# Attention's product with the values turned round, and its row sums taken by a column of ones

## The chip, the cores and the metric

The kernel runs on one core of one Trainium2 chip. A core has a matrix engine (TensorE, PE in the profile, with its weight loads listed as PEld), a vector engine (VectorE, DVE), a scalar engine (ScalarE, ACT), a general engine (GpSimd, POOL), a synchronisation engine that here only issues transfers (SyncE, SP), and 16 DMA engines that move data between the chip's memory and the core's SBUF. Results of TensorE land in PSUM, of which this kernel uses all eight banks (2 KB for each of 128 partitions). Each engine works through its own list of instructions in order; across engines an instruction waits for what it needs by semaphores. The metric is the device time of one execution, in microseconds. All data here are float32.

## The reference: what is computed

The reference is an attention with a band and a few global keys, followed by a mixture of eight experts in which each token goes to one expert:

```python
# B, H, S, D = 4, 8, 768, 64; n_global, n_local = 8, 96
scores = scale * q @ k.T                       # per batch and head
keep   = (pos_k < n_global) | (0 <= pos_q - pos_k < n_local)
dist   = where(global and not local, n_local, |pos_q - pos_k|)
scores = where(keep, scores - slope[h] * dist, -1e9)
a = exp(scores - max); a = a / sum(a)
x = (a @ v) as (B*S, H*D)                      # 3072 tokens of 512 numbers
logits = x @ w_gate                            # 512 x 8
e = argmax(logits); g = softmax(logits)[e]
y = g * relu(x @ w1[e]) @ w2[e]                # 512 x 1024 and 1024 x 512
```

## The kernel before

**Stages.** Three stretches follow one another: the attention of four batches (about 11 to 161 us of the profile), a tail in which the last tokens are routed while the first tokens of expert 0 are already worked on (161 to 217 us), and the other experts' matrix products (217 to 509 us). The order in each engine's list is the order in which the program is written: nothing reorders it.

**Units and rounds.** A *unit* is one batch `b`, one pair of heads `j` (four pairs) and two tiles of 128 queries (`c` = 0, 1, 2): 48 units, 12 a batch. A query tile sees only its own key block and one other (`kA`, the block before, with the 16 first keys in place of its first 16), so a unit has four 128x128 blocks of scores for each head (three where `c` is 0). The loop takes two units a *round*. In a round the lists get: `turn_qk` (VectorE's 32x32 transposes for the next pair of heads, L462), `scores` of both units (TensorE `s` L508; the exponential on ScalarE L514 into `e`; the product with the weights of distance on VectorE L521 and L525), `turn` of the units of two rounds before, `attend` of the units of the round before, now and then a step of the routing, then ScalarE's copies that make the next pair's shifted keys (`keys_at`, L427, L429) and values (`turn_v`, L453, L454), and the loads of later pairs (`load`, `load_v`), which SP issues.

**`attend` and `turn`.** `attend` multiplies with the exponentials `e` as the stationary operand and the values as the moving one. The values carry a column of ones, so that the sum of each row of `e` comes out beside the product; the moving operand is 128 columns wide, of which the 65 first are used. VectorE takes the reciprocals of the sums (L547), multiplies (L550) and so leaves finished `x` in `xr`, token by row. `turn` transposes `xr` on TensorE (`px`, L560), ScalarE copies the result (L562) into `w2_f`, a stretch of SBUF that later holds expert 1's second weights, and once a pair of heads is the last, `store` (L252) writes the rows of `x` to the table `x_tok` in the chip's memory, from which the experts gather their tokens.

**Routing.** Once a batch, in the round with `m` = 2 of the next batch (`m` counts units within a batch): `logits` multiplies the transposed `x` by the gate matrix on TensorE (`pq`, L574, in column groups of 32), VectorE transposes, `gate` finds each token's expert, with one exponential on ScalarE (`ex`, L233). `spread` (a product `pr` with a triangle of ones), `tables` (VectorE: `oh`, L624) and `spread_sum` (`pi`, L633) turn this into each token's place in its expert's list; they follow at `m` = 4, 6 and 8, or 4, 4 and 6 for the last batch that the loop serves.

**The tail.** After the loop the last batch goes through the same steps. Between them `work(1)` puts a piece of expert 0's product (`ph` L346 with its relu L341, and `po` L354) into TensorE's list, so that it has something to do while VectorE routes. Expert 0's weights (`w_first`; L760 and L762) are loaded by SP in pieces, one at a time from unit 12 on; expert 1's 4 MB (`w_second`, in whose place attention keeps its operands) are issued by SP in the tail. GpSimd gathers the rows of `x_tok` by index for each expert.

**PSUM.** `ps_s` holds the scores (two tiles of two banks), `ps_o` the product (two of one bank), `ps_m` everything else (two of one bank).

## Time and profile before

| | |
|---|---|
| time, median of 3 runs | 518.11 us (517.02 to 518.5) |
| the profiled execution, its own time | 518.61 us |
| its span in the profile | 516.7 us |
| granted TensorE clock, mean | 0.996 |
| TensorE busy | 500.3 us, 97% |
| weight loads (beside TensorE) | 346.6 us, 67% |
| VectorE busy | 181.4 us, 35% |
| ScalarE busy | 127.4 us, 25% |
| GpSimd busy | 137.9 us, 27% |
| TensorE busy of the attention's 150 us (11 to 161) | 148.6 us |
| VectorE, ScalarE busy in the same stretch | 121.0 us, 89.7 us |
| TensorE busy of the tail's 56 us (161 to 217) | 55.9 us |
| TensorE busy of the experts' 292 us (217 to 509) | 291.1 us |
| memory read, written | 59.0 MB, 12.75 MB |

The span runs from the first to the last instruction that the profile shows; 1.9 us of the execution's own time lie around it. The experts' stretch keeps TensorE at work all the time, and so do the attention and the tail. TensorE's records overlap, because its products are pipelined; a float32 product is two records ("x2"). In the lines shown below, the chain of the work that ended last has a start and a duration, the engine, the output's name, the line and the number of records; the timeline has a start, a duration, the engine, the line, the operation, the output and inputs with their sizes, the number of records, and in brackets a wait with what ended it.

### The profile page before, as it was taken

To read this page: it belongs to the slowest core of one execution; us is meant where nothing else is said; L and a number is where in the kernel's file an instruction comes from. 1 tells how busy PE (TensorE), PEld (TensorE's weight loads), DVE (VectorE), ACT (ScalarE), POOL (GpSimd) and SP (SyncE) were. 2 spreads that over 40 slices of the span, in tenths; PEclk is the share of its full clock that TensorE was granted. 3 is DMA by queue.
4 is the path that set the end of the run, shared out by engine and by line. 5 is a ranking of instruction groups with operands and counts; after the bars stand their busy time and mean duration, and the time that the engine had idled before them with its cause. 6 is when DMAs were issued, how large, how long until landed. Compare 5 with 4: busy or idle time off the path is not lost.

```text
span 516.7 us, 7988 instructions
## 1 busy us (share of the span) xinstructions
PE 500.3 (97%) x3108; PEld 346.6 (67%) x3108; DVE 181.4 (35%) x484; ACT 127.4 (25%) x227; POOL 137.9 (27%) x161
## 2 busy tenths in 40 slices
PE   4999999999999999999999999999999999999993
PEld 3999999999999949955455455545545746545541
DVE  5878797897884532310300120030012021020010
ACT  4776656656651102011002001101100201101100
POOL 5000000000024266543353244244025526310010
PEclk9999999999999999999999999999999999999998
DMA  9998999999937911963751826466083576010001
GB/s 153 160 171 154 238 178 172 226 173 171 290 99 215 273 38 45 229 219 71 165 179 62 159 82 203 85 147 210 4 192 88 175 185 213 22 42 18 1 23 41
DMA packets 145183, 71.95 MB, mean 139 GB/s; under 512 B 126672, under 2 KB 126678, under 8 KB 145136
## 3 DMA queue, kind: packets, MB, share of 16 engines
q1 hardware_dynamic: 137344, 58.16, 48.8%
q0 software_dynamic: 5264, 12.59, 8.1%
q10 hardware_dynamic: 2528, 0.59, 0.7%
q8 instruction: 26, 0.43, 0.4%
q14 instruction: 21, 0.17, 0.1%
HBM read 59.00 MB, written 12.75 MB: 139 GB/s over the span
## 4 chain that ended last, share of the span: by engine, by line
PE 87%; POOL 3%; DMA 3%; DVE 3%; issue 2%; SPq 1%; POOLq 0%; ACT 0%
PE ph L1066 28%; PE po L1123 27%; PE o L543 14%; PE s L508 8%; PE px L560 2%; PE ph L346 2%; POOL xq_s L288 2%; DMA xq_s<-x_tok,rows 2%; PE pt L1132 1%; PE po L354 1%; PE pq L574 1%; PE pi L633 1%; DMA w_first<-in_moe_w_dram 1%; PE first L443 1%; SPq L252 0%
## 5 line engine op out<-in xcount | busy, mean ns | idle before, releaser
L1068 ACT ACTIVATE hT<-ph 128x416 f32<-128x416 f32 (+4 forms) x64 | 29.9, 467 | 278.0 <-PE ph L1066 278.0
L334 DVE TENSOR_SCALAR y<-po,gslot_s 128x512 f32<-128x512 f32 (+1 forms) x17 | 12.8, 751 | 215.4 <-PE po L1123 215.4
L288 POOL DMA_INDIRECT xq_s<-x_tok,rows_s x72 | 72.6, 1008 | 58.3 <-ACT hT L1068 42.7
L1066 PE MATMUL ph<-xe,w_second 128*128 128x416 f32 (+3 forms) x256 | 79.4, 470 | 0.3 <-DVE xe L299 0.3
L1123 PE MATMUL po<-w_second,hT 128*128 128x512 f32 (+1 forms) x176 | 76.2, 592 | 0.0
L1066 PE MATMUL ph<-xe,w_first 128*128 128x208 f32 (+3 forms) x256 | 75.8, 457 | 0.1
L1066 PEld LDWEIGHTS ph<-xe,w_second 128*128 128x128 f32 x256 | 48.3, 190 | 29.7 <-issue 10.4
L1066 PEld LDWEIGHTS ph<-xe,w_first 128*128 128x128 f32 x256 | 47.5, 190 | 27.6 <-issue 10.7
L1123 PE MATMUL po<-w_first,hT 128*128 128x512 f32 (+1 forms) x144 | 62.3, 592 | 0.0
L1123 PEld LDWEIGHTS po<-w_second,hT 128*128 128x128 f32 (+1 forms) x176 | 33.2, 189 | 41.3 <-issue 40.7
L288 POOL DMA_INDIRECT xq<-x_tok,rows x15 | 15.7, 1044 | 163.1 <-DVE rows L271 158.0
L543 PE MATMUL o<-vt,e 128*128 128x128 f32 x288 | 53.9, 278 | 0.0
L326 POOL DMA_INDIRECT out_dram<-y,idx_s x17 | 17.2, 1010 | 124.9 <-DVE xe L299 72.0
L1123 PEld LDWEIGHTS po<-w_first,hT 128*128 128x128 f32 (+1 forms) x144 | 27.2, 189 | 34.0 <-issue 33.5
L543 PE MATMUL o<-va,e 128*128 128x128 f32 x240 | 46.9, 277 | 0.0
L543 PEld LDWEIGHTS o<-vt,e 128*128 128x128 f32 x288 | 43.1, 195 | 0.2 <-issue 0.2
L514 ACT ACTIVATE e<-s 128x1024 f32<-128x1024 f32 (+1 forms) x36 | 33.4, 947 | 31.5 <-PE s L508 31.3
L508 PE MATMUL s<-qT,kT 64*128 64x128 f32 x384 | 38.8, 286 | 0.9 <-ACT qT L445 0.9
L543 PEld LDWEIGHTS o<-va,e 128*128 128x128 f32 x240 | 36.9, 194 | 0.1
L508 PE MATMUL s<-qT,kA 64*128 64x128 f32 x320 | 34.2, 292 | 2.0 <-ACT kA L429 2.0
L525 DVE TENSOR_TENSOR e<-e,Wb 128x1024 f32<-128x1024 f32 x24 | 28.8, 1212 | 9.3 <-ACT e L514 9.0
L508 PEld LDWEIGHTS s<-qT,kT 64*128 64x128 f32 x384 | 30.2, 196 | 2.2 <-ACT qT L445 1.3
(189 smaller groups left out, 503.1 us busy)
## 6 DMA issues: line engine op xcount, KB each, us to landing
w_second<-in_moe_w_dram SPq DMA_DIRECT2D x16, 512.0 KB, 8.4
w_second<-in_moe_w_dram SPq DMA_DIRECT2D x4, 2048.0 KB, 9.7
x_tok<-xr SPq DMA_DIRECT2D x24, 256.0 KB, 3.9
w_first<-in_moe_w_dram SPq DMA_DIRECT2D x12, 512.0 KB, 8.6
w_first<-in_moe_w_dram SPq DMA_DIRECT2D x3, 2048.0 KB, 9.9
vt<-in_v_dram SPq DMA_DIRECT2D x31, 192.0 KB, 3.8
w_second<-in_q_dram SPq DMA_DIRECT2D x60, 96.0 KB, 3.3
w_second<-in_k_dram SPq DMA_DIRECT2D x60, 96.0 KB, 2.8
```

The costliest lines, as they stand in the source:

```text
L288: return nc.gpsimd.indirect_dma_start(out=xq[:, i, :], out_offset=None, in_=x_tok[0:NJ * top, :], in_offset=bass.IndirectOffsetOnAxis(ap=c ...
L326: p = nc.gpsimd.indirect_dma_start(out=to[:, :], out_offset=bass.IndirectOffsetOnAxis(ap=where, axis=0), in_=y[0:rows, :], in_offset=None, ...
L334: done = nc.vector.tensor_scalar(out=y[0:rows, :], in0=po[0:rows, :], scalar1=gs[0:rows, :], scalar2=None, op0=ALU.mult)
L346: done = nc.tensor.matmul(ph[:, P * f:P * f + P], lhsT=w1_0[:, 0, kc, c0:c0 + P], rhs=xe_0[:, kc, P * q:P * q + P], start=(kc == 0), stop= ...
L508: nc.tensor.matmul(ps[:, h, P * m:P * m + P], lhsT=lhsT, rhs=qT[r, P * i:P * i + P], start=True, stop=True)
L514: nc.scalar.activation(e[:, :, 0:w], ps[:, :, 0:w], AF.Exp, scale=D ** -0.5)
L525: nc.vector.tensor_tensor(out=eh, in0=eh, in1=W[:, 2 * j:2 * j + 2, P:3 * P].rearrange("p h (o c) -> p h o c", o=1).to_broadcast([P, 2, 2, ...
L543: nc.tensor.matmul(po[:, t, h, :], lhsT=pt[:, h, P * m:P * m + P], rhs=(vt if own else va)[:, c0:c0 + P], start=(m == mine[0][0]), stop=(m ...
L560: nc.tensor.transpose(px[:, 2 * i + t, :], xrs[b, c][:, t, P * j:P * j + P], ident)
L1066: nc.tensor.matmul(ph[:, 0:C], lhsT=w1t[:, 0, kc, P * fc:P * fc + P], rhs=xe[:, kc, 0:C], start=(kc == 0), stop=(kc == KC - 1))
L1068: done = nc.scalar.activation(hT[:, fc, 0:C], ph[:, 0:C], AF.Relu)
L1123: nc.tensor.matmul(po[0:rows, :], lhsT=hT[:, fc, P * q:P * q + rows], rhs=w2t[:, 0, fc, :], start=(fc == 0), stop=(fc == FC - 1))
```

## The change

`attend` is turned round: the values are the stationary operand (64 columns) and `e` the moving one. The two heads of a pair go into the two column halves of the array, so `po` is `x` transposed, 64 rows a head, one after the other by heads; ScalarE copies it into `w2_f` (L550), unscaled. Its PSUM is now one bank for both units of a round (`po_all`), and the bank that this leaves free collects sums (`pc_all`). The row sums come from four further products a unit: a stationary operand of 32 columns (`one_of`, a column of ones at a place that depends on the unit), one of four column quarters for each head and key block, `e` 256 wide; the sums of a whole batch pile up in one bank, one row a unit. `turn` now transposes from `w2_f` to token by row, and two copies of ScalarE bring it into `xr`, still unscaled.

Once a batch ScalarE copies the sums out (`sums_out`), TensorE transposes them into an unused part of the last scores' banks, VectorE adds the two key blocks' shares and takes the reciprocals (`recip_of`). The gate's products are made per pair of heads, with each head's columns apart (`partials`, `pl`), copied to SBUF, transposed back (`pq`), multiplied by the reciprocals and added up (`logits`), and `finish_x` scales the three `xr` of a batch on VectorE and stores them. The loop places these at `m` = 0, 2 and 8 of the next batch (4 for the last that it serves). In the tail the stores come after `tables`, and expert 1's weights after the stores. Expert 0's weights start six units later, and what is left of them is issued after the loop. The values lose their column of ones, and GpSimd the filling of it (these edits aren't in the cut below); token numbers, reciprocals and gate matrix change their layout. Lines of the kernel after: `s` L497, exponential L503, `o_all` L532, `c_all` L548, its copy L550, `px` L557, copies L562, `sums_out` L568, transposes L573, `partials` L587, `pq` L600, `finish_x` L619, expert 0's relu L341.

```diff
-            ps_o = actx.enter_context(tc.tile_pool(name="ps_ob", bufs=2, space=PSUM))
+            ps_o = actx.enter_context(tc.tile_pool(name="ps_ob", bufs=1, space=PSUM))
             ps_m = actx.enter_context(tc.tile_pool(name="ps_mb", bufs=2, space=PSUM))
-
-            VW = D + 1
+            ps_c = actx.enter_context(tc.tile_pool(name="ps_cb", bufs=1, space=PSUM))
+
+            po_all = ps_o.tile([P, 2, 2, P], F32, tag="o", name="o_all")
+            pc_all = ps_c.tile([P, 2, 2, P], F32, tag="c", name="c_all")
...
+            one_of = vp.tile([P, 2 * 32 - 1], F32, name="one_of")
+            nc.vector.memset(one_of, 0.0)
+            nc.vector.memset(one_of[:, 31:32], 1.0)
...
-                po = ps_o.tile([P, 2, 2, P], F32, tag="o", name=f"o_{n}")
+                po = po_all[:, n % 2, :, :]
                 for t in range(2):
                     mine = [(m, own) for m, (u, own) in enumerate(bl) if u == t]
-                    for h in range(2):
-                        for m, own in mine:
-                            i = 2 * c + t
-                            c0 = VT * h + VW * i if own else VA * h + VW * (i - 1)
-                            nc.tensor.matmul(po[:, t, h, :], lhsT=pt[:, h, P * m:P * m + P],
-                                             rhs=(vt if own else va)[:, c0:c0 + P],
-                                             start=(m == mine[0][0]), stop=(m == mine[-1][0]))
-                r = recips[:, 2 * n:2 * n + 2, :]
-                nc.vector.reciprocal(r.rearrange("p t (h o) -> p t h o", o=1), po[:, :, :, D:D + 1])
-                if j == 0:
-                    xrs[b, c] = xrp.tile([P, 2, DM], F32, tag="xr", name=f"xr_{b}_{c}")
-                nc.vector.tensor_tensor(
-                    out=xrs[b, c][:, :, P * j:P * j + P].rearrange("p t (h d) -> p t h d", h=2), in0=po[:, :, :, 0:D],
-                    in1=r.rearrange("p t (h o) -> p t h o", o=1).to_broadcast([P, 2, 2, D]), op=ALU.mult)
+                    for m, own in mine:
+                        i = 2 * c + t
+                        for h in range(2):
+                            nc.tensor.matmul(po[D * h:D * h + D, t, :], lhsT=vt[:, h, i, :] if own else va[:, h, i - 1, :],
+                                             rhs=pt[:, h, P * m:P * m + P], start=(m == mine[0][0]), stop=(m == mine[-1][0]))
+                m = n % nb
+                pc = pc_all[:, b % 2, :, :]
+                r = NJ * c + j
+                for own in (1, 0):
+
+                    lots = [(1, 2)] if c == 0 and not own else [(0, 1), (1, 2)] if m == 1 and not own else [(0, 2)]
+                    for t0, t1 in lots:
+                        for h in range(2):
+                            g = 2 * h + own
+                            if c == 0 and not own:
+                                rhs = pt[:, h, P:2 * P].rearrange("p (t q) -> p t q", t=1)
+                            else:
+                                k = own if c > 0 else 0
+                                rhs = pt[:, h, :].rearrange("p (t k q) -> p k t q", k=2, q=P)[:, k, t0:t1, :]
+                            nc.tensor.matmul(pc[32 * g:32 * g + 32, t0:t1, :], lhsT=one_of[:, 31 - r:63 - r], rhs=rhs,
+                                             start=(m == 0), stop=(m == nb - 1))
+                nc.scalar.copy(out=w2_f[:, 2 * P * m:2 * P * m + 2 * P], in_=po.rearrange("p t q -> p (t q)"))
 
             def turn(n):
 
                 px = ps_m.tile([P, 4, P], F32, tag="m", name=f"px_{n}")
+                for i in range(4):
+                    o = 2 * P * (n % nb) + P * i
+                    nc.tensor.transpose(px[:, i, :], w2_f[:, o:o + P], ident)
                 for i in range(2):
                     b, j, c = units[n + i]
-                    for t in range(2):
-                        nc.tensor.transpose(px[:, 2 * i + t, :], xrs[b, c][:, t, P * j:P * j + P], ident)
-                m = n % nb
-                nc.scalar.copy(out=w2_f[:, 2 * P * m:2 * P * m + 4 * P], in_=px.rearrange("p t c -> p (t c)"))
-                for i in range(2):
-                    b, j, c = units[n + i]
-                    if j == NJ - 1:
-                        store(S * b + 2 * P * c, 2, xrs.pop((b, c)))
+                    if j == 0:
+                        xrs[b, c] = xrp.tile([P, 2, DM], F32, tag="xr", name=f"xr_{b}_{c}")
+                    nc.scalar.copy(out=xrs[b, c][:, :, P * j:P * j + P], in_=px[:, 2 * i:2 * i + 2, :])
+
+            gl = w1_f[:, 4 * S:5 * S].rearrange("p (c t q) -> p c t q", t=2, q=P)
+            sums = w1_f[:, 5 * S:5 * S + 2 * P].rearrange("p (t q) -> p t q", t=2)
+
+            def sums_out(b):
+                nc.scalar.copy(out=sums, in_=pc_all[:, b % 2, :, :])
+
+            def recip_of(b, pr):
+
+                for t in range(2):
+                    nc.tensor.transpose(pr[:, t, :], sums[:, t, :], ident)
+                to = recips[:, b, :, :, :].rearrange("p t c h -> p t (c h)")
+                for t in range(2):
+                    nc.vector.tensor_reduce(
+                        out=to[:, t, :].rearrange("p (r h) -> p h r", h=2),
+                        in_=pr[:, t, :].rearrange("p (h o r) -> p h r o", h=2, o=2)[:, :, 0:nb, :], axis=AX.X, op=ALU.add)
+                nc.vector.reciprocal(to, to)
+
+            def partials(b, c0, c1):
+
+                pl = ps_m.tile([P, c1 - c0, 2 * P], F32, tag="m", name=f"pl_{b}_{c0}")
+                for c in range(c0, c1):
+                    for j in range(NJ):
+                        o = 2 * P * (NB // 2 * j + c)
+                        nc.tensor.matmul(pl[32 * j:32 * j + 32, c - c0, :], lhsT=wg_sb[:, j, :], rhs=w2_f[:, o:o + 2 * P],
+                                         start=True, stop=True)
+                nc.scalar.copy(out=gl[:, c0:c1, :, :].rearrange("p c t q -> p c (t q)"), in_=pl)
 
             def logits(b):
 
-                xl = w2_f[:, 0:KC * S].rearrange("p (k t) -> p k t", k=KC)
-                pq = ps_m.tile([P, QS], F32, tag="m", name=f"pq_{b}")
-                for kc in range(KC):
-                    for g in range(TB):
-                        nc.tensor.matmul(pq[32 * g:32 * g + 32, :], lhsT=wg_sb[:, kc, :], rhs=xl[:, kc, QS * g:QS * g + QS],
-                                         start=(kc == 0), stop=(kc == KC - 1))
-                L = gp.tile([P, QS], F32, tag="L", name=f"L_{b}")
-                nc.vector.transpose(L, pq)
-                gate(b, L.rearrange("p (c w) -> p c w", w=32)[:, :, 0:E], gp,
-                     M_b[b][:, :, 1:NB + 1].rearrange("p e c -> p c e"))
+                tmp = gp.tile([P, NB * P], F32, tag="oh", name=f"tmp_{b}", bufs=1)[:, 0:NB * H * E].rearrange(
+                    "p (i h e) -> p i h e", h=H, e=E)
+                tiles = [(t, c) for t in range(2) for c in range(NB // 2)]
+                for i0, i1 in ((0, 4), (4, NB)):
+                    pq = ps_m.tile([P, i1 - i0, NJ, 32], F32, tag="m", name=f"pq_{b}_{i0}")
+                    for i in range(i0, i1):
+                        t, c = tiles[i]
+                        nc.tensor.transpose(pq[:, i - i0, :, :].rearrange("p j w -> p (j w)"), gl[:, c, t, :], ident)
+                    n = (i1 - i0) * NJ
+                    r = recips[:, b, :, :, :].rearrange("p t c (j h) -> p (t c j) h", h=2)
+                    nc.vector.tensor_tensor(
+                        out=tmp[:, i0:i1, :, :].rearrange("p i (j h) e -> p (i j) h e", h=2),
+                        in0=pq.rearrange("p i j w -> p (i j) w")[:, :, 0:2 * E].rearrange("p n (h e) -> p n h e", h=2),
+                        in1=r[:, NJ * i0:NJ * i1, :].rearrange("p n (h o) -> p n h o", o=1).to_broadcast([P, n, 2, E]), op=ALU.mult)
+                L = gp.tile([P, NB, E], F32, tag="L", name=f"L_{b}")
+                nc.vector.tensor_reduce(out=L, in_=tmp.rearrange("p i h e -> p i e h"), axis=AX.X, op=ALU.add)
+                gate(b, L, gp, M_b[b][:, :, 1:NB + 1].rearrange("p e c -> p c e"))
                 nc.vector.tensor_tensor_scan(out=C_b[b].rearrange("p e c -> p (e c)"), data0=first0.rearrange("p e c -> p (e c)"),
                                              data1=M_b[b].rearrange("p e c -> p (e c)"), initial=0.0, op0=ALU.mult, op1=ALU.add)
                 if b < B - 1:
                     nc.vector.tensor_copy(out=M_b[b + 1][:, :, 0:1], in_=C_b[b][:, :, NB:NB + 1])
...
+            def finish_x(b, c):
+
+                xr = xrs.pop((b, c))
+                x4 = xr.rearrange("p t (h d) -> p t h d", h=H)
+                nc.vector.tensor_tensor(out=x4, in0=x4, in1=recips[:, b, :, c, :].rearrange("p t (h o) -> p t h o", o=1)
+                                        .to_broadcast([P, 2, H, D]), op=ALU.mult)
+                store(S * b + 2 * P * c, 2, xr)
...
-                    if n % 3 > 0 and n >= 12:
+                    if n % 3 > 0 and n >= 18:
...
+                if b > 0 and m == 0:
+                    partials(b - 1, 0, 1)
+                if b > 0 and m == 2:
+                    recip_of(b - 1, st["ps"][:, :, 3 * P:4 * P])
+                    partials(b - 1, 1, NB // 2)
                 if n0 >= 4:
                     turn(n0 - 4)
                     for n in two:
                         attend(n - 2)
                         if n == nu - 4:
                             fetch_0(0)
+                if b > 0 and m == 0:
+                    sums_out(b - 1)
                 if b > 0 and m == 2:
                     logits(b - 1)
                 if b > 0 and m == 4:
                     spread(b - 1)
+                if b > 0 and m == (4 if b == B - 1 else 8):
+                    for i in range(NB // 2):
+                        finish_x(b - 1, i)
...
             attend(nu - 2)
             turn_x(xe_0, xq_0[0], TB)
+            partials(B - 1, 0, 1)
             turn(nu - 4)
             attend(nu - 1)
+            sums_out(B - 1)
             turn_x(xe_0[:, :, P:2 * P], xq_0[1], TB)
+            while weights_0:
+                weights_0.pop(0)()
+            st["ph"], st["po"] = (ps_s.tile([P, 2, 512], F32, tag="s", name=f"{i}_0") for i in ("ph", "po"))
             work(1)
             count_0()
+            recip_of(B - 1, st["ph"][:, 0, 2 * P:4 * P].rearrange("p (t q) -> p t q", t=2))
             turn(nu - 2)
-            expert_w1(w1_1, slice(1, 2))
+            partials(B - 1, 1, NB // 2)
             work(1)
             logits(B - 1)
-            nc.sync.dma_start(w2_1, w2v[:, 1:2, :, :])
+            finish_x(B - 1, 0)
             work(1)
             spread(B - 1)
             tables(B - 1)
+            for i in range(1, NB // 2):
+                finish_x(B - 1, i)
+            expert_w1(w1_1, slice(1, 2))
+            nc.sync.dma_start(w2_1, w2v[:, 1:2, :, :])
```

## The prediction

> **What bounds the kernel now.** First the busy sums, then the chain that ended last, because a busy TensorE is not yet a TensorE at its rate.
>
> ```profile
> PE 500.3 (97%) x3108; PEld 346.6 (67%) x3108; DVE 181.4 (35%) x484; ACT 127.4 (25%) x227; POOL 137.9 (27%) x161
> ```
>
> In the chain (start, duration) one round of two units is scores `s`, transposes `px`, products `o`:
>
> ```profile
> 52.55 3.13 PE o L543 x28
> 55.67 1.44 PE pq L574 x32
> 57.11 1.99 PE s L508 x32
> 59.09 0.58 PE px L560 x4
> 59.68 3.13 PE o L543 x28
> ...
> 261.68 1.88 PE pt L1132 x64
> ```
>
> The rows meet end to end and TensorE has no waits of weight after 24 us: the attention stage (about 11 to 161 us) runs at TensorE's rate. A float32 product is two records (passes). `o` takes 3.13/28 = 0.112 us a pass; `s`, whose two heads lie in different row halves, two passes in 0.112; `pt`, four column quarters, four passes in 1.88/16 = 0.118. So products in different parts of the array run together.
>
> The TensorE timeline of one round shows the price of changing from one partition of the array to another:
>
> ```profile
> 124.63 0.39 PE L543 MATMUL o<-vt,w_second 128*128 128x128 f32 x2
> 124.95 0.49 PE L508 MATMUL s<-qT,kA 64*128 64x128 f32 x4
> 125.28 0.39 PE L508 MATMUL s<-qT,kT 64*128 64x128 f32 x4
> ...
> 126.39 0.39 PE L508 MATMUL s<-qT,kT 64*128 64x128 f32 x4
> 126.71 0.66 PE L560 MATMUL px<-ident,xr 128*128 128x128 f32 x4
> 127.21 0.61 PE L543 MATMUL o<-vt,e 128*128 128x128 f32 x4
> ```
>
> The last `o` pass starts at 124.63 + 0.11 = 124.74, `s` at 124.95: 0.21 for 0.11, and the first pass of `s` is another 0.10 longer (0.49 against 0.39): 0.20 for the change. `s` to `px`: 0.10 + 0.05. `px` to `o`, both the whole array, costs nothing. By the same reading `o` to `pq` (32 columns) is 0.12.
>
> Then ScalarE, which is not critical here, in the round after a batch's logits:
>
> ```profile
> 58.07 0.24 ACT L233 ACTIVATE ex<-L 128x48 f32<-128x48 f32 x1 [4.53 <-DVE L L231]
> 58.22 0.72 ACT L453 COPY va<-vt 128x650 f32<-128x650 f32 x1
> 58.97 0.63 ACT L454 COPY va<-vt 16x520 f32<-16x520 f32 x1
> 59.51 1.91 ACT L514 ACTIVATE e<-s 128x1024 f32<-128x1024 f32 x2
> 61.33 0.56 ACT L562 COPY w_second<-px 128x512 f32<-128x512 f32 x1
> ```
>
> It waits for VectorE's gate until 58.07, so its `px` copy comes at 61.33, 1.6 us after TensorE went on to `o` (59.68). Before, nothing on TensorE asks for ScalarE in between; the change makes it ask.
>
> **What the Trainium skill says.** "TensorEngine Tiling (Array Packing)", Tiling Modes, Key Properties: changing the tiling mode drains the TensorE. The 0.10 to 0.20 us above agree; that column halves against column quarters is such a change, no row of before shows. The same page, Performance Considerations, PSUM Bottleneck: tiling speeds TensorE but not the evacuation of PSUM. "PSUM — Partial Sum Buffer", Terms: TensorE must not write a bank (and quadrant) while another engine reads it. "TensorE: Matmul & The Clock Gate", Part 1, Architectural detail: ScalarE and VectorE are strict FIFO; the `ex` row agrees.
>
> **The change part by part** (against the profiled 518.6 us, 0.5 above the median of 518.1).
>
> *Products.* 704 passes at 0.112 become 352 pairs of column halves. Before has no 64-column row; bounds are 0.112 (row halves) and 0.118/2 x 2 = 0.118 (quarters): I take 0.112, at most +2 us. 704 x 0.112 - 352 x 0.112 = **-39.3**.
>
> *Sums.* Each unit adds four products of 32 columns, 256 wide, in four quarters. `pq` (192 wide, four abreast) takes 0.1625 a pass of four, so 256 wide 0.216, two passes 0.43; 48 units: **+20.7**. If the four run only two abreast it is twice that.
>
> *Changes of tiling.* A round was s, px, o: two changes. It becomes s, px, halves, quarters, halves, quarters. Halves entered: 0.09 drain plus about 0.05 for a weight load that can't run ahead, 0.14; quarters 0.12. (0.14 + 0.12) x 2 = 0.52 x 24 rounds = **+12.6**. Lower end 0 (halves and quarters mix freely, and are entered free), upper 0.20 each: 19.
>
> *Logits.* `pq` goes (1.44 a batch). In come 24 quarter passes of 256 (6 groups x 0.216 = 1.3), two transposes for the sums and six for the partials (8 x 0.11 = 0.9), changes 0.7: 2.9, **+1.5 x 4 = +6.1**. TensorE's own time is then +0.1: the halved product is spent on sums and drains.
>
> *Waits on ScalarE.* `po_all` is one bank, and as ordered every odd unit's first product waits for ScalarE's copy (L550) of the even unit just before; behind it stands the rest of TensorE's queue. From the last product pass the copy needs 0.32 (pass end and signal) + 0.37 (`qT<-first`, 128x256 out of PSUM, 0.372) + 0.05 = 0.74; the sums and two changes cover 0.76. So it is hidden only while ScalarE is free. After units with c = 1, 2 it first does keys (0.8) and values (1.3): exp starts 1.9 us after the scores instead of 1.2, the copy ends at 4.4 where TensorE would go on at 3.9: 0.56, twice a batch (once 0.26); in the first batch also W's exponentials (L476): 2.2 + 3 x 0.8 = **+4.6**. In the second round of a batch the sums' transposes write the bank of the last scores and wait for its exp: 1.1 x 3 = **+3.3**. In the round after logits `ex` comes later than before (two multiplies and a 384-element reduction, about 1.2 us, for a 0.38 transpose), at 1.7 after the scores start; then values 1.3, two exps 1.8, two copies 0.5, the copy at 5.4 to 5.8 against 4.1: 1.7 x 3 = **+5.1**.
>
> *VectorE.* It loses 48 reciprocals and multiplies (0.55 each) and gains 12 scalings of 128x1024 (like L525, 1.21). Mostly hidden. Not in the last batch, where three scalings stand between `spread` and `tables`, in a stretch where VectorE is back to back:
>
> ```profile
> 141.65 0.95 DVE L624 TENSOR_TENSOR oh<-iota_p,lo 128x768 f32<-128x768 f32 x1
> 142.52 0.97 DVE L462 STREAM_TRANSPOSE kT<-w_second 128x768 f32<-128x768 f32 x1
> ```
>
> `oh` is what TensorE's `pi` takes: +3.4 less 1.1 for multiplies gone, +0.6 for the longer logits, less 1.7 that TensorE is already late: **+1.2**.
>
> *Tail.* Sums' transposes wait for a relu on `ph`'s bank (0.5), `pr` for the longer gate (0.4), `pi` for one scaling (0.6): **+1.5**. The stores of the last batch move behind `tables`, on SP ahead of expert 1's 4 MB, and the gathers behind them: first gather some 3 us later, beside those 4 MB. There is little slack, as the chain shows:
>
> ```profile
> 206.08 11.12 DMA xq_s<-x_tok,rows
> 217.59 3.06 PE ph L1066 x8
> ```
>
> A gather beside a weight load takes 11 us there. Bounds 0 and 6; I take **+1**.
>
> *At nothing.* The POOL fills of ones that go (0.4 us of memsets), the shifted weight pieces on SP (four of 128 KB behind attention; `w_first` is used from 161 us, pieces of `w2` not until 180), and the loads of q, k and v, issued almost back to back on SP: a slower attention gives them more room. If attention became 10 us shorter they would have to be delivered in 120 us instead of 130, about what SP's 12 us of waits leave; then they would bind.
>
> Sum: 0.1 + 4.6 + 3.3 + 5.1 + 1.2 + 1.5 + 1 = +16.8: 535.4 profiled, **535** as a median.
>
> **The rivals.** *No helper is late* (0.12): ScalarE and VectorE deliver before TensorE asks. For it: before, TensorE lost 0.1 us to them in 150. Against it: the copy has 0.02 us of slack. It decides once all waits together fall under 1.6 us; then only TensorE's +0.1 remains, 518: not slower, and faster where drains are cheaper too. *Tilings mix freely* (0.17): -12.6 and -1.4 in the logits; but TensorE reaches the copy 0.2 us early every round (4.8), so about 526. For it: no row shows halves to quarters. *Sums run two abreast* (0.08): +20.7, 556; `pq` and `pt` speak against it. *The tail's gathers stall the experts* (0.13): +6 to +10, 543. Mine keeps 0.50.
>
> **How the numbers follow.** About 0.3% (1.6 us) is what a measurement can tell from no change. Faster: two thirds of "no helper late", 0.08; same 0.05; slower 0.87. The range leaves out sums two abreast (0.08) and half of the no-wait case: 516 to 550. The likeliest case alone: 527 to 545.
>
> **What would show it.** `o_all` pairs every 0.11 us (products right); `c_all` groups of four every 0.22 (sums); about 0.2 us from the last pass of one tiling to the first of the next, twice per unit more (changes); TensorE idle before L532 put down to L550, most after `ex`; idle before L573 put down to L503; attention's last product about 13 us later than 160.6. I am wrong if halves run one after the other, if the copies never bind, or if the experts (217 to 509 us) change length by more than their start.

## The result and the profile after

The changed kernel takes 540.3 us in the median against 518.3; the ratio is 1.041 (95% interval 1.035 to 1.047), some 21 us. In this document the medians include, and the ratios leave out, two executions in a slower state: one of the changed kernel's four here (549.2 us at a granted clock of 0.972) and one of experiment 12's twelve (650.6 us at 0.757). Forecast were 535, with a range of 516 to 550. Timed again on another chip beside the kernel before (experiment 8) it came to 540.6 against 520.0, 1.040 (1.038 to 1.042). The profiled execution took 542.7 us with a span of 541.0, at a granted clock of 0.984 where before has 0.996; this last number turns out to matter.

The first part of the profile's page, columns as before:

```profile
PE 508.8 (94%) x3508; PEld 319.6 (59%) x3508; DVE 176.0 (33%) x420; ACT 148.8 (28%) x311; POOL 136.8 (25%) x153
```

TensorE has 400 records more and its share falls from 97% to 94%: it now waits. ScalarE has gained 21 us. The chain that ended last (start, duration), from the transposed sums of a batch to the round after its logits:

```profile
96.68 0.71 ACT w_second L503
97.87 1.00 PE pl L587 x16
...
103.05 0.63 DVE tmp L603 x2
...
105.21 0.72 ACT va L444
106.48 1.91 ACT e L503 x2
109.22 0.88 PE o_all L532 x12
```

Before, such a stretch was TensorE alone, row after row. Now the chain passes through the scores' exponential (L503) to the transposed sums, later through VectorE's multiply and reduction into ScalarE's values, and comes back to TensorE only at 109.22.

A steady round of the changed kernel on TensorE's timeline:

```profile
84.91 0.44 PE L532 MATMUL o_all<-e,va 128*64 128x128 f32 x4
85.18 0.39 PE L532 MATMUL o_all<-e,vt 128*64 128x128 f32 x4
85.40 0.39 PE L532 MATMUL o_all<-e,va 128*64 128x128 f32 x4
...
85.94 0.64 PE L548 MATMUL c_all<-e,one_of 128*32 128x256 f32 x8
86.50 0.44 PE L532 MATMUL o_all<-e,vt 128*64 128x128 f32 x4
```

Four records of `o_all`, two pairs of column halves, take 0.22 us: 0.11 a pair. The unit's eight pairs would be 0.90 and last 1.03 (84.91 to 85.94), so the change to quarters costs 0.13; its two groups of four sums would be 0.43 and last 0.56 (to 86.50), 0.13 again. That is 0.26 a unit, the forecast's number.

TensorE's waits in that execution (total us, times, longest), cut to the largest that the change brought:

```profile
PE o_all L532 <- ACT w_second L550: 8.1, 6, 1.8
...
PE s L573 <- ACT w_second L503: 3.0, 3, 1.0
...
PE ph L339 <- ACT hT L341: 0.9, 2, 0.5
...
PE po L347 <- DVE y L327: 0.8, 1, 0.8
```

ScalarE in the round after a batch's logits, the answer to the rows shown of before:

```profile
105.06 0.24 ACT L226 ACTIVATE ex<-L 128x48 f32<-128x48 f32 x1 [2.80 <-DVE L L224]
105.21 0.71 ACT L444 COPY va<-vt 128x640 f32<-128x640 f32 x1
...
106.48 1.91 ACT L503 ACTIVATE e<-s 128x1024 f32<-128x1024 f32 x2
...
108.82 0.36 ACT L550 COPY w_second<-o_all 128x256 f32<-128x256 f32 x1
```

ScalarE stands still for 2.8 us until VectorE has the logits, then works without a pause, in order: values, exponentials, `px`, and only then the copy L550, for which TensorE has waited since 107.4. This is the 1.8 us stall, once a batch.

From the start times in the traces the span divides into three parts (attention: first scores to the end of the last unit's products or sums; tail: from there to the first product of the other experts, L1066 before and L1123 after; experts: the rest). This tail ends at 194 us before, earlier than the one in the table of the profile before (161 to 217):

| us | attention | tail | experts |
|---|---|---|---|
| before (clock 0.996) | 154.1 | 33.2 | 322.7 |
| changed, first profile (0.984) | 172.5 | 39.2 | 322.3 |
| changed, experiment 8 (0.997) | 168.0 | 39.7 | 322.3 |

At full clock the change costs 13.9 in attention, 6.0 to 6.5 in the tail and nothing in the experts.

### The profile page after: what moved, and what is told of

The parts are those of the page before. It is cut to its first block, busy times and chain, and to the rows that moved or that the text cites. A ratio compares the mean times of both kernels' runs of the same rounds, so it can differ in the third digit from the quotient of the medians.

```text
span 541.0 us, 8835 instructions
## 1 busy us (share of the span) xinstructions
PE 508.8 (94%) x3508; PEld 319.6 (59%) x3508; DVE 176.0 (33%) x420; ACT 148.8 (28%) x311; POOL 136.8 (25%) x153
## 4 chain that ended last, share of the span: by engine, by line
PE 85%; ACT 5%; SPq 4%; DVE 2%; DMA 1%; issue 1%; POOL 0%; POOLq 0%; ACTq 0%
PE ph L1123 29%; PE po L1180 25%; PE o_all L532 7%; PE s L497 5%; PE c_all L548 4%; SPq L404 3%; PE po L347 3%; PE ph L339 3%; PE po L1160 2%; PE px L557 2%; ACT e L503 2%; PE pt L1189 1%; PE pl L587 1%; PE pi L671 1%; ACT kA L420 1%
## 5 line engine op out<-in xcount | busy, mean ns | idle before, releaser
L327 DVE TENSOR_SCALAR y<-po,gslot_s 128x512 f32<-128x512 f32 (+1 forms) x17 | 12.8, 751 | 215.4 <-PE po L1180 215.4
L1123 PE MATMUL ph<-xe,w_second 128*128 128x416 f32 (+3 forms) x256 | 79.4, 470 | 0.0
L1123 PE MATMUL ph<-xe,w_first 128*128 128x208 f32 (+3 forms) x256 | 76.0, 457 | 1.0 <-DVE y L327 0.8
L1123 PEld LDWEIGHTS ph<-xe,w_second 128*128 128x128 f32 x256 | 48.3, 190 | 29.3 <-issue 10.4
L1123 PEld LDWEIGHTS ph<-xe,w_first 128*128 128x128 f32 x256 | 47.4, 190 | 28.8 <-issue 10.3
L1180 PEld LDWEIGHTS po<-w_second,hT 128*128 128x128 f32 (+1 forms) x176 | 33.2, 189 | 41.3 <-issue 40.7
L497 PE MATMUL s<-qT,kT 64*128 64x128 f32 x384 | 40.7, 298 | 0.9 <-ACT qT L438 0.9
L497 PE MATMUL s<-qT,kA 64*128 64x128 f32 x320 | 36.6, 309 | 2.8 <-ACT kA L422 2.8
L503 ACT ACTIVATE e<-s 128x1024 f32<-128x1024 f32 (+1 forms) x36 | 33.0, 944 | 10.0 <-PE s L497 9.9
L497 PEld LDWEIGHTS s<-qT,kT 64*128 64x128 f32 x384 | 32.1, 208 | 3.6 <-issue 1.6
L497 PEld LDWEIGHTS s<-qT,kA 64*128 64x128 f32 x320 | 27.2, 208 | 8.9 <-ACT kA L422 4.0
L532 PE MATMUL o_all<-e,vt 128*64 128x128 f32 x288 | 29.1, 281 | 0.0
L532 PE MATMUL o_all<-e,va 128*64 128x128 f32 x240 | 24.9, 287 | 2.0 <-ACT w_second L550 2.0
L550 ACT COPY w_second<-o_all 128x256 f32<-128x256 f32 x48 | 18.0, 376 | 30.2 <-PE o_all L532 29.8
```

Of the source, the lines that this page charges most:

```text
L497: nc.tensor.matmul(ps[:, h, P * m:P * m + P], lhsT=lhsT, rhs=qT[r, P * i:P * i + P], start=True, stop=True)
L503: nc.scalar.activation(e[:, :, 0:w], ps[:, :, 0:w], AF.Exp, scale=D ** -0.5)
L532: nc.tensor.matmul(po[D * h:D * h + D, t, :], lhsT=vt[:, h, i, :] if own else va[:, h, i - 1, :], rhs=pt[:, h, P * m:P * m + P], start=(m ...
L550: nc.scalar.copy(out=w2_f[:, 2 * P * m:2 * P * m + 2 * P], in_=po.rearrange("p t q -> p (t q)"))
L1123: nc.tensor.matmul(ph[:, 0:C], lhsT=w1t[:, 0, kc, P * fc:P * fc + P], rhs=xe[:, kc, 0:C], start=(kc == 0), stop=(kc == KC - 1))
L1180: nc.tensor.matmul(po[0:rows, :], lhsT=hT[:, fc, P * q:P * q + rows], rhs=w2t[:, 0, fc, :], start=(fc == 0), stop=(fc == FC - 1))
```

## The experiments

Each is compared with runs of the kernel before on its own chip; "attention" and "tail" are the parts above, from its own trace.

| | time / before | ratio (95%) | attention | tail | clock, profiled |
|---|---|---|---|---|---|
| 1 rotation of three banks | 534.7 / 519.5 | 1.029 (1.027 to 1.030) | 164.5 | 39.2 | 0.989 |
| 2 sums' transposes later | 543.2 / 519.5 | 1.045 (1.041 to 1.048) | 171.1 | 39.2 | 0.978 |
| 3 the tail's tiles apart | 537.8 / 519.5 | 1.035 (1.033 to 1.037) | 166.9 | 36.0 | 0.996 |
| 4 rotation, products grouped | 529.3 / 519.5 | 1.020 (1.017 to 1.023) | 155.8 | 39.2 | 0.997 |
| 5 all mended | 525.0 / 520.0 | 1.011 (1.009 to 1.014) | 156.2 | 35.4 | 0.991 |
| 6 before, with three stalls | 530.4 / 520.0 | 1.022 (1.020 to 1.025) | 163.0 | 34.0 | 0.992 |
| 7 sums of batch 0 alone | 530.0 / 520.0 | 1.018 (1.014 to 1.022) | 156.8 | 40.7 | 0.983 |
| 8 the changed kernel again | 540.6 / 520.0 | 1.040 (1.038 to 1.042) | 168.0 | 39.7 | 0.997 |
| 9 all mended, values on GpSimd | 528.3 / 520.4 | 1.015 (1.012 to 1.018) | 164.1 | 35.4 | 0.982 |
| 10 all mended, copies on VectorE | 526.4 / 520.4 | 1.011 (1.008 to 1.015) | 160.2 | 34.9 | 0.986 |
| 11 both of these | 538.7 / 520.4 | 1.035 (1.031 to 1.038) | 172.6 | 34.9 | 0.982 |
| 12 values on GpSimd, two orders mended | 523.3 / 520.1 | 1.006 (1.004 to 1.008) | 151.6 | 38.8 | 0.994 |

**1. A bank of its own for each unit's product.** Against the changed kernel:

```diff
-            ps_o = actx.enter_context(tc.tile_pool(name="ps_ob", bufs=1, space=PSUM))
-            ps_m = actx.enter_context(tc.tile_pool(name="ps_mb", bufs=2, space=PSUM))
+            ps_m = actx.enter_context(tc.tile_pool(name="ps_mb", bufs=3, space=PSUM))
...
-                po = po_all[:, n % 2, :, :]
+                po = ps_m.tile([P, 4, P], F32, tag="m", name=f"o_{n}")[:, 0:2, :]
```

> Products of the two units of a round in different PSUM banks: the product's tile comes from the common rotation, which gets three banks, so no product waits for ScalarE's copy of the unit just before. Theory (the shared tile sets the wait): the 8.1 us of waits of L532 for L550 in the trace go, the wait of the sums' transposes for the exponential (3.0) stays; 532 against 540, about 8 less. Rival (ScalarE is itself too late in those rounds): the wait moves to the next thing that asks for ScalarE, the transposes px or the next scores, and the time falls by less than 3 us. A second rival (the clock is what is lost): waits go, but the granted clock stays at 0.984 to 0.995 and takes a part back.

Of TensorE's waits in it:

```profile
PE pi L669 <- DVE oh L660: 1.5, 1, 1.5
```

The products' wait is gone from the list, the one for the exponential (3.0) is still there. The ratio falls from 1.040 (experiment 8) to 1.029, 5.8 us of the 8: TensorE now comes earlier to the routing's tables and waits 1.5 for `oh`, where it waited 0.6 or not at all. The shared tile set the wait, as the theory said; ScalarE caught up in most rounds. Whether the copy L550, placed earlier in ScalarE's list, would have done the same was not tried.

**2. The sums' transposes later.**

```diff
                 if b > 0 and m == 2:
-                    recip_of(b - 1, st["ps"][:, :, 3 * P:4 * P])
                     partials(b - 1, 1, NB // 2)
...
                 if b > 0 and m == 2:
+                    recip_of(b - 1, st["ps"][:, :, 3 * P:4 * P])
                     logits(b - 1)
```

> The sums' transposes and reciprocals are moved in the loop from just after the scores to just ahead of the logits, so that the exponential of those scores is long done. Theory: the 3.0 us of waits for L503 go; but the reciprocals come 0.5 us later with respect to the multiplies, so the gate's exponential is as late as before and the 1.8 us stall of L532 in the next round grows by up to 0.5 each time: net 1.5 to 3 us less, 537 to 539. Rival (TensorE would have been held there anyway, by VectorE or ScalarE): no change, the wait stands at the px transposes instead.

```profile
PE o_all L532 <- ACT w_second L550: 8.8, 5, 2.3
```

The wait for L503 went and this stall grew from 1.8 to 2.3, both as expected; the time did not fall. What took the gain back is the clock: 0.976 to 0.984 in the four runs, among the lowest of all. In this trace it is at 0.50 in four stretches, 20.5 us together, three of them after the three stalls of 2.3 us; attention is 171.1 long, 3.1 more than at full clock in experiment 8, although its waits are 2.7 us shorter. A miss, and the first sign that stalls cost more than their length.

**3. The tail's tiles apart.**

```diff
-                return hidden_0(st["ph"][:, f0 // 2 % 2, 0:2 * P], z, f0, 2)
+                ph = ps_s.tile([P, 2, 512], F32, tag="s", name=f"ph_0_{z}_{f0}")
+                return hidden_0(ph[:, 0, 0:2 * P], z, f0, 2)
...
-                return result_0(st["po"][:, z, :], z, f0, 2, later)
+                if f0 == 0:
+                    po = ps_o.tile([P, 2, 2, P], F32, tag="o", name="po_0_0") if z == 0 else ps_c.tile([P, 2, 2, P], F32, tag="c", name="po_0_1")
+                    st["po"] = po.rearrange("p a t q -> p (a t q)")
+                return result_0(st["po"], z, f0, 2, later)
...
-            recip_of(B - 1, st["ph"][:, 0, 2 * P:4 * P].rearrange("p (t q) -> p t q", t=2))
+            recip_of(B - 1, ps_m.tile([P, 2, P], F32, tag="m", name="pr_last"))
```

> In the tail alone: expert 0's hidden pieces take a new tile of two from the scores' pool each time, its two results have a bank of their own each, and the last batch's sums are transposed into a tile of their own. Theory (what was late in the tail is TensorE behind its own evacuations, because one tile of two banks is waited for as a whole): the waits for the relu L341 (0.9 and 0.4) and for the scaling L327 (0.8 and 0.8) go, the tail from the last sums to the experts' first product falls from 39.2 to about 36.4 us, 2.9 less in all. Rival (the gathers or the routing set the end of the tail): the same time appears as a wait for xe or for the tables, tail 39.

TensorE's waits between 175 and 215 us:

```profile
PE pr L628 <- DVE se L236: 0.9, 1, 0.9
```

The waits for L341 and L327 (0.8 each of `po` and of the experts' first `ph`) are gone, a wait of 0.7 for `early` is new, and the tail is 36.0. The two halves of `ph` and of `po` lie in different banks, yet as built a product into one half waits for the reading of the other: in the first profile the piece that ends at 192.06 is read by ScalarE from 192.10 on, and the next piece, in the other half, starts only at 192.54. The tile is waited for as a whole, and that was 3.2 us.

**4. Both units' products, then both units' sums**, on top of 1 (`attend` with `apart` leaves the sums, which `sums_of` then does):

```diff
                     for n in two:
-                        attend(n - 2)
+                        attend(n - 2, apart=True)
+                    for n in two:
+                        sums_of(n - 2)
```

> As with the rotation of three banks, and besides in each round both units' products first and then both units' sums: one entry into column halves and one into quarters a round instead of two. Theory (each change of tiling costs TensorE 0.12 to 0.14 us): 0.26 less a round, 5.5 to 6 us below the rotation alone, about 526. Rival (halves and quarters mix freely, and what is seen at the change is only the modelled end of a record): no difference to the rotation alone.

```profile
84.87 0.44 PE L530 MATMUL o<-e,va 128*64 128x128 f32 x4
...
86.77 0.64 PE L554 MATMUL c_all<-e,one_of 128*32 128x256 f32 x8
87.22 0.61 PE L554 MATMUL c_all<-w_second,one_of 128*32 128x256 f32 x8
87.77 0.49 PE L495 MATMUL s<-qT,kA 64*128 64x128 f32 x4
```

Products and sums of a round of full units take 2.90 us (84.87 to 87.77) where the ungrouped kernel takes 2 x (1.03 + 0.56) = 3.18: 0.28 less. In time it is 5.4 us below the rotation alone, about 0.25 for each of the 22 rounds that are grouped. So the time at a change of tiling (the drain, in which TensorE empties before it goes on) is real, and not only a modelled end of a record.

**5. All of it**: 1 to 4, and `finish_x` of the last batch in the loop after `tables`, `count_0` later in the tail.

> All the mended waits together on the turned product: rotation of three banks, both units' products ahead of both units' sums, the sums' transposes just ahead of the logits, expert 0's pieces in tiles of their own, and for the last batch that the loop serves the scaling of x after the tables; the count of expert 0's tokens in the tail comes after the tables. Theory (what made the change slower were waits, two changes of tiling a round too many and the tail's shared tiles): the grouped kernel's 529 less 3.0 (wait for L501), 1.8 (wait for oh), 2.9 to 3.6 (tail), so 520 to 522, within 0.5% of before on this chip. Rival (each gap that closes opens another one behind it, as the rotation's 8 us became 6): 525.

```profile
PE pi L676 <- ACT xr L567: 1.9, 1, 1.9
```

525.0, the rival's number; each gap that closed opened another. With the rotation the routing's tiles come free only when ScalarE has copied `px` out, and ScalarE is late by that much.

**6. The kernel before, with stalls put in.** In three rounds the transposes take their identity from a fresh copy of ScalarE's:

```diff
+            late = mp.tile([P, P], F32, name="late")
...
+                held = n >= 12 and n % 12 == 0
+                if held:
+                    nc.scalar.copy(out=late, in_=ident)
+                    nc.scalar.copy(out=late, in_=ident)
...
-                        nc.tensor.transpose(px[:, 2 * i + t, :], xrs[b, c][:, t, P * j:P * j + P], ident)
+                        nc.tensor.transpose(px[:, 2 * i + t, :], xrs[b, c][:, t, P * j:P * j + P], late if held else ident)
```

> The kernel before, with three stalls put into TensorE and nothing else changed: at m = 4 of batches 1 to 3 the transposes px use a copy of the identity that ScalarE makes twice over just before, behind its exponentials. Each stall should be 1.6 to 3 us, so +5 to +9 in all. Theory of the clock (a stall of TensorE of about 2 us inside full work is followed some 3.5 us later by a stretch of halved clock): the granted clock falls from 0.996 to 0.985 or so in several of the runs, and the time rises by up to 5 us more than the stalls. Rival (it is the turned product itself, or the chip's chance, that lowers the clock): the clock stays at 0.994 to 0.997.

```profile
102.53 1.11 PE L566 MATMUL px<-late,xr 128*128 128x128 f32 x4 [2.90 <-ACT late L562]
103.43 0.64 PE L543 MATMUL o<-va,e 128*128 128x128 f32 x2
103.86 0.63 PE L543 MATMUL o<-vt,e 128*128 128x128 f32 x2
```

After the stall of 2.9 us the very products that take 0.22 a pair of passes elsewhere in this kernel take 0.43, until about 105.6. Busy times by window (PE, PEld, DVE, ACT, POOL, granted clock, DMA share, GB/s) show the same as a mean clock of 0.57 over 4 us, of which 3.4 are at 0.50:

```profile
102.00:106.00 4.00, 3.47 (x18) 3.47 (x19) 2.30 (x3) 1.74 (x5) 0.00 (x0) 0.57 0.92 209
```

One of the three stalls did this; after the other two the clock stayed full. The stalls sum to 8.7 us and the time rose by 10.4; the clock is 0.986 to 0.992 in the four runs against 0.992 to 0.998 for the kernel before beside it. So it is not the turned product that lowers the clock: a stall of TensorE is enough, and not every time. The size, some 2 us, is well within the 5 that was thought possible. Why one stall of three did it is taken up in the last section.

**7. Sums of batch 0 for all batches**, on top of 1 (the kernel leaves out the sums' products of batches 1 to 3, so their `x` is divided by the wrong sums):

```diff
-                for own in (1, 0):
+                for own in (1, 0) if b == 0 else ():
...
```

> The rotation of three banks, with the sums' products of batches 1 to 3 left out: the sums of batch 0 stand in for theirs. Theory (sums cost 0.43 us a unit and two changes of tiling 0.26): 36 x 0.69 = 25 less than the rotation alone, about 510 if nothing else comes to bind; the products turned round would then be a gain of 9 us against before. Rival (helpers or loads bind once TensorE is faster, ScalarE above all, whose copies, exponentials and keys take about 5 us of a round of 4.6): 515 to 522, with TensorE's waits on ScalarE back.

A miss for the theory, and above the rival's 515 to 522 too: 5.6 us below the rotation (by the ratios) in place of 25. Taken from one start to the next without the waits, TensorE's own time in attention falls by 19.6 us, but its waits there rise from 8.4 to 20.3, and 10.6 us of it run at half the clock where the rotation's trace has 6.8 (clock 0.977 to 0.988 in the four runs). The longest in the list, of which 2.0 are at the start, as in every run here:

```profile
PE s L495 <- ACT kA L420: 5.1, 10, 2.0
```

TensorE was the bound by a small margin. Once it is faster, it waits at once for ScalarE's keys and copies.

**8. The changed kernel again.**

> The changed kernel as it is, on the same chip as the others, for its granted clock: theory of the clock: in its four runs 0.976 to 0.996, with the halved stretches following the stalls of 1.8 us; otherwise as before, 537 to 543.

```profile
PE o_all L532 <- ACT w_second L550: 7.9, 6, 1.8
```

Its waits are nearly those of the first profile, but its clock is 0.992 to 0.997: the stalls of 1.8 us are there, the slowed stretches aren't, and the change costs 4% without them.

**9 to 11. Work moved off ScalarE**, on top of 5: the values' copies to GpSimd (9), the products' copies to VectorE (10), both (11).

```diff
-                nc.scalar.copy(out=va, in_=vt[:, :, 0:NB - 1, :])
+                nc.gpsimd.tensor_copy(out=va, in_=vt[:, :, 0:NB - 1, :])
...
```

> All the mended waits together, and besides the two copies that make the next pair's values (1.35 us a pair, 22 us in all) move from ScalarE to GpSimd, which has nothing to do in attention. Theory (ScalarE is what is late in the rounds after the logits): TensorE's waits on ScalarE's copies, 4.9 us in the trace with all mended waits, fall to about 1, the time by 3 to 4 us, to 521. Rival (GpSimd's copies are slow and come late themselves, or slow VectorE down): a wait of the products for va, or VectorE's multiplies longer than 1.21, and no gain.

> All the mended waits together, and besides the copies of the products (L533, 18 us in all) move from ScalarE to VectorE. Theory: ScalarE is relieved by as much as with GpSimd, but VectorE is back to back in the rounds of the routing, so the transposes px that need these copies wait for it there: 522 to 525. Rival (only ScalarE's queue counts): 521.

> Both moves at once, values to GpSimd and the products' copies to VectorE: ScalarE keeps the exponentials, the keys and the copies of px. Theory: not better than the move to GpSimd alone, as VectorE then sets the end: 521 to 523.

GpSimd's queue in 9:

```profile
151.85 1.23 POOL L281 DMA_INDIRECT xq<-x_tok,rows  x1 [7.47 <-DMA w_first<-in_moe_w_dram]
...
162.66 0.73 POOL L442 COPY va<-vt 128x640 f32<-128x640 f32 x1
```

TensorE's waits there, and in 11:

```profile
PE o L530 <- POOL va L442: 8.2, 2, 7.8
PE px L562 <- DVE w_second L533: 5.7, 6, 1.6
```

In 9 TensorE's waits on ScalarE did go, but the last pair's values stand behind eight gathers which themselves wait 7.5 us, and the last products wait 7.8 for them: 528.3 where 521 was expected. With the copies on VectorE nothing is gained (526.4, the 1.011 of experiment 5, and above the 522 to 525 expected). Both together are the slowest of the three, 538.7 where 521 to 523 was expected: the wait for the values stays, and `px` waits 5.7 us for VectorE.

**12. Two orders mended in 9**: the last pair's values stay on ScalarE, two scalings of `x` come a round later.

```diff
+                copy = nc.gpsimd.tensor_copy if pr < B * NJ - 1 else nc.scalar.copy
...
-                if b > 0 and m == (4 if b == B - 1 else 8):
-                    for i in range(NB // 2):
+                if b > 0 and m in ((4, 6) if b == B - 1 else (8,)):
+                    for i in range(NB // 2) if m == 8 else (0,) if m == 4 else (1, 2):
```

> The values on GpSimd, but the last pair's on ScalarE, because GpSimd's queue then stands behind the gathers of expert 0, which wait for the stores of x; and two of the three scalings of the last batch that the loop serves one round later, behind the transposes of the last pair. Theory (the 7.8 us wait of the products for va and the 1.8 us wait of the scores for qT in the run before were these two orders, and nothing else is late): 528.3 less 8 to 9.6, so 519 to 520.5, the same as before. Rival (the late gathers then hold the tail, or the clock falls again): 522 to 525.

Attention has hardly a wait left and takes 151.6, 2.5 less than before the change. But the total is 0.6% above before, in the range of the rival (522 to 525) and not of the theory. The tail, 38.8, has lost what attention won:

```profile
160.65 0.31 DVE L292 STREAM_TRANSPOSE xe<-xq 128x128 f32<-128x128 f32 x1 [1.07 <-DMA xq<-x_tok,rows]
161.15 0.49 PE L339 MATMUL ph<-xe,w_first 128*128 128x128 f32 x3 [0.69 <-issue]
```

Expert 0's first piece follows its tokens one gather at a time, 1.3 us apart, and takes 5.2 us in place of 1.9; the mean granted clock from 160 to 164 and from 164 to 168 is 0.84 and 0.73. No version of the turned product was found that is faster than the kernel before.

## Why the prediction was right, and where it was not

The forecast was slower by 16.8 us for the reason that came true: TensorE wins 39 us of products, spends them on sums and drains, and then waits for ScalarE. Measured were some 21 on the first chip (the ratio of 1.041) and 20.6 in experiment 8 at full clock. Some products in the working are off by 0.1 (704 less 352 passes at 0.112 are 39.4, not 39.3; 0.52 x 24 is 12.5, not 12.6), on which nothing turns. By its steps, measured in experiment 8's trace against that of before, from one start on TensorE to the next:

- *Products, sums and changes* (forecast -6.0): -5.3. Products and sums take 74.4 where the products took 81.5, and `px`, which now ends with a change too, takes 1.8 more (0.08 in each of 23 rounds). The passes and the changes are as taken. Grouping confirmed the drains by removing half of them.
- *Logits of three batches* (+4.6): +4.5.
- *The copy L550*: forecast 9.7 in attention, measured 7.9, but otherwise divided. The round after the logits: 1.83 three times, 5.5 for 5.1. The first batch: 1.3 for 2.2 (2.4 in the first profile). The keys and values in later batches: a single wait of 1.1, behind the last pair's values, for 2.4 (0.2 in the first profile). This step was over-sized; in the other rounds ScalarE kept the small slack that the working gave it.
- *The sums' transposes* (+3.3): 3.0. *VectorE in the last batch* (+1.2): 0.6.
- Not in the sum: 3.2 in attention, of which waits for the keys' copies are 0.9, the scores themselves 1.7 (48.5 for 46.8), for which no reason was looked for, and the routing's products the rest.
- *Tail* (logits 1.5, waits 1.5, gathers 1; 4.0 together): 6.0 to 6.5. In the first profile the sums' transposes wait 0.4 for the relu and `pr` 0.8 for the gate, about as forecast, and `pi` not at all; the gathers cost the experts nothing, as their 322.3 shows. The term left out is larger: products that wait for the relu and the scaling of the piece before, 2.6 us in four waits, because `ph` and `po` became one tile each. With these waits gone experiment 3's tail is 3.2 shorter, although a new one of 0.7 came up. The forecast saw that dependence in `po_all` and took it for one of the bank; experiment 3 shows that it is one of the tile, since these halves lie in two banks. A look at the two new tiles in the tail would have given it.
- So the total came nearer than its parts: the copy was over-sized by 1.8 and VectorE by 0.6, while the tail was 2.0 to 2.5 short and 3.2 were in no step. In part that is luck.
- *The clock* was taken as unchanged. In the first profile it lost 1.2%, and attention is 4.5 longer than in experiment 8. Three stretches at 0.50, 13.7 us together, hold the loss; the second of these windows of 4 us covers one of them:

```profile
107.00:111.00 4.00, 2.17 (x32) 1.21 (x24) 4.00 (x6) 3.02 (x8) 0.00 (x0) 1.00 0.36 61
111.00:115.00 4.00, 4.00 (x35) 3.63 (x33) 3.61 (x10) 2.70 (x6) 0.00 (x0) 0.57 0.71 112
```

The 1.8 us stall is in the first, the slowed scores in the second; the next is at full clock again. That a stall is enough is shown by the kernel before with stalls put in (experiment 6); for this kernel it rests on the count over all traces in the last section.

The rivals: *no helper late* is out (11 us of waits in attention). *Tilings mix freely* is out (0.13 each, and experiment 4). *Sums two abreast* is out (four every 0.22). *Gathers stall the experts* is out; they held the tail only in experiment 12, where attention ended 17 us earlier.

## What to carry to other kernels

When a product on a full TensorE gets shorter, count first what else TensorE will now ask for: the drains of each new tiling, and every engine that so far had time to spare. Batch products of one tiling before going to the next, and give each accumulator that another engine reads a tile of its own, or one half will wait for the other. In this kernel ScalarE was busy for 60% and VectorE for 81% of attention beside a full TensorE, and with even most of the sums left out (experiment 7) the turned product was not faster; where the helpers are that full, look at them before making TensorE's share shorter.

## What the runs showed that was not expected

A stall of TensorE (time in which it has nothing to do) can cost more than its length. The Trainium skill ("TensorE: Matmul & The Clock Gate", HAM oscillation — how this bites in real kernels) warns of idle gaps over about 3.4 us, after which the array runs at half its clock. Here stalls of 1.5 to 2.9 us inside full work were followed by stretches of 3.4 or 6.8 us at a clock of 0.50, in some executions and not in others: the kernel before had a clock of 0.992 to 0.998 in all its runs, kernels with such stalls 0.972 to 0.997, and the last experiment, whose tail is chopped by shorter waits, 0.985 to 0.998 in all but one. The measurement decides: shorter gaps can suffice.

Which stalls do it depends in good part on where they fall. The clock records of the fourteen traces have 20 slowed stretches ahead of the last one at each kernel's end, and within a trace all of them start at whole multiples of 3.41 us from one another. So each trace can be laid out in cells of 3.41 us, and TensorE's idle time counted in each cell that is at full clock:

| idle in the cell | cells | followed by a cell at 0.50 |
|---|---|---|
| under 1.37 us | 2011 | 0 |
| 1.37 to 1.92 us | 21 | 10 |
| over 1.92 us | 10 | 10 |

The limits of the rows are where the answers change. A stall that straddles two cells is shared out between them. In the first profile the stalls at 30.7, 107.4 and 150.2 us put 1.81, 1.45 and 1.84 us into one cell, and each was followed by a slowed stretch; the equally long one at 66.1 was divided into 0.68 and 1.15, and was not. In experiment 6 the three stalls put 1.92, 2.59 and 1.80 into one cell, and only the second slowed the clock; in experiment 8 the three after the logits put 1.71, 1.41 and 1.11, and none did; experiment 2's longer stalls put 2.31, 2.31 and 1.82, and all did. This is a count over runs that were made for other reasons, and no stall was placed on purpose; what decides between 1.37 and 1.92 us stays open.

GpSimd's copies of the values took 1.00 and 0.93 us in experiment 9 where ScalarE's take 0.72 and 0.62 in the changed kernel (means of 16), quick enough to take this work over as long as no gather stands before them: in experiment 12 TensorE waited 0.4 us for them in all.
